# A filtered sequence and its mixture of experts on one core: first group of expert 0 in halves, and another order in the last batch

## The chip, the cores and the metric

The program runs on one core of a Trainium2 chip: TensorE (PE) for matmuls and transposes, VectorE (DVE), ScalarE (ACT), GpSimd (POOL), SyncE (SP) which only issues transfers, and 16 DMA engines. The metric is the device time of one execution in microseconds (us). The times of before are those of three runs, and one further execution was profiled; every row below is from that one.

## What is computed

Eight sequences of 2496 tokens with 256 channels are filtered in the frequency domain, and the result goes through a mixture of eight experts in which every expert takes exactly cap = 2496 tokens, given out in the order of the logits over all tokens:

```python
X = np.fft.rfft(x, axis=1);  Y = X * F[None]          # F = filt_r + 1j * filt_i
y = np.fft.irfft(Y, n=2496, axis=1).reshape(19968, 256)
logits = y @ w_gate
for idx in np.argsort(-logits.flatten()):              # greedy, largest logit first
    tok, e = idx // 8, idx % 8
    if assigned[tok] < 0 and counts[e] < cap:
        assigned[tok] = e; counts[e] += 1
for e in range(8):
    m = assigned == e
    out[m] = np.maximum(y[m] @ w1[e], 0.0) @ w2[e]
```

## The kernel before

**The transforms.** A length of 2496 is split as 39 x 64. Each of the eight batches goes through `s1` (L209) and `s2` (L224), is multiplied with the filter (products `P` and `Q` on VectorE at L230 and L231, their sums on GpSimd at L232 and L233, all in `s2`), is transposed (`tr`, ten tiles `q` per batch, L243), and goes through the first inverse stage `inv1` (L279), whose tile `zt` ScalarE copies (L293) and stores to a scratch tensor `zd` in DRAM (two stores on ScalarE's queue, L296, with two `zt` buffers). The second inverse stage `inv2` loads units `z<-zd` of 120 partitions x 5 x 256 numbers (614 KB; each batch has four such and one of 2 x 256 numbers, 246 KB) on SyncE's queue (L362), multiplies them with `cD` (L395), copies them (L396), and stores `xs<-xo` on ScalarE's queue. The first two batches' units run inside the loop over the batches; those of the other six, 30 units called `rest`, run after the last batch.

**The logits.** They are computed in the frequency domain, ahead of `inv2`: gate products (L252, in `tr`), their copy `vs`, `trv` (L271, a high part `Vh` by ScalarE and a remainder `Vl` by VectorE), and `v1` (L314), `v2` (L330), `v3` (L340) into `lg`. The seven first batches go through `v1` to `v3` together while the last is transformed, the last batch alone behind it. `prep` (L536 to L543, VectorE) makes the routing's first operands `M`, `Gm` and `A` of `lg`.

**The routing.** Eleven threshold rounds (`counts`: matmuls L567 and L580) run among the matmuls of `inv2`; `places` (L758 to L780: one-hot tiles `OH`, matmuls L764, ScalarE pieces `junka` L768, then small VectorE pieces) turns the result into lists of tokens, one list for each chunk of 512 tokens of an expert.

**The experts.** Each expert has five groups of tokens (4 x 512 and 448). GpSimd gathers the rows (`xg`, L823, four gathers per group), `turn` transposes them (L837; two halves of 256 tokens, ScalarE makes the high part `xo` at L840, VectorE the remainder `z` at L841), `first` makes 8 products `pz` of 6 matmuls, 512 columns wide (L859), of which ScalarE makes the relu's high part (L865) and VectorE its remainder (L873), `second` makes `py` (L913, L914), and GpSimd scatters. `split` makes high and low parts of weights (L816, L817). Accumulators `pz` have four buffers.

**What sets the order.** Outside `manual_schedule` the events of `run` are sorted by slot (ten slots to a batch, B = 8 batches) and then by priority, and a scheduler with its own model puts the instructions in each engine's order. Inside `manual_schedule` (from the routing's rounds on) TensorE's order is that of the code, and the other engines' that of the scheduler. `issue_after(x)` has an instruction ordered behind x. `Pump` deals out the routing's pieces by a clock of its own. Between the last `inv2` unit and the first transpose of expert 0, 24 constant matmuls (`rest`, L1015) run.

## Time and profile before

| | |
|---|---|
| runs | 1471.03, 1453.58, 1469.07 us (median 1469.07) |
| profiled execution | 1465.58 us, of which the span from the first instruction to the last is 1463.8 us |
| granted TensorE clock, mean | 0.982 |
| PE busy | 1391.3 us (95%) |
| DVE, ACT, POOL busy | 955.6, 723.7, 663.6 us |
| DMA | 149.17 MB |

Times in rows are in microseconds from the start of the span. A row of a timeline has the start, the duration, the engine, line and operation, output and inputs by the program's names, and, in brackets, how long the engine stood idle before it and what released it. `SPq`, `ACTq` are issues of transfers, whose duration is that of the issuing, not of the transfer.

### The profile page before, as it was taken

The page shows a single profiled execution, that of the slowest core. Times are in us where ns is not written, and L with a number is a line of the kernel's source. Part 1 is how long each engine was busy: PE and PEld are TensorE (multiplying, and loading weights), DVE is VectorE, ACT ScalarE, POOL GpSimd, SP SyncE. Part 2 cuts the span into 40 slices and gives each one's busy share as a digit, 9 for nine tenths or more (in the row PEclk, how much of TensorE's full clock was granted, in tenths as well). Part 3 has the DMA queues.
Part 4 walks back from the last instruction along what each step waited for, and adds up shares of the span by engine and source line. Part 5 has one row for each costly group of instructions (what it writes and reads, how often), then busy time and mean ns, then how long its engine had stood idle before and what let it go on. Part 6 is the DMA issues. An engine that isn't in the chain of part 4 may idle for free. (4 is left out here: it accounts for less than half of the span.)

```text
span 1463.8 us, 24844 instructions
## 1 busy us (share of the span) xinstructions
PE 1391.3 (95%) x9127; PEld 1148.7 (78%) x9127; DVE 955.6 (65%) x2574; ACT 723.7 (49%) x1686; POOL 663.6 (45%) x729
## 2 busy tenths in 40 slices
PE   7899999998997999899999899999999999999998
PEld 6889899776445787677778788787878888888887
DVE  5666676576566789666876976977877854432231
ACT  5666677534473345344544533644553654533332
POOL 5433344243004745553664546366545644445423
PEclk9999999999998999999999999999999999999999
DMA  8554454888892102112110211211211221111100
GB/s 263 185 148 143 126 163 116 237 239 206 328 348 74 51 22 95 53 35 75 59 52 25 98 49 39 90 51 48 95 37 50 102 95 52 38 48 46 42 26 27
DMA packets 54780, 149.17 MB, mean 102 GB/s; under 512 B 9258, under 2 KB 29866, under 8 KB 50706
## 3 DMA queue, kind: packets, MB, share of 16 engines
q0 software_dynamic: 17552, 57.72, 12.1%
q1 hardware_dynamic: 9803, 47.11, 10.6%
q10 hardware_dynamic: 27304, 42.76, 9.5%
q8 instruction: 72, 1.18, 0.3%
q14 instruction: 49, 0.40, 0.1%
HBM read 83.89 MB, written 63.70 MB: 101 GB/s over the span
## 5 line engine op out<-in xcount | busy, mean ns | idle before, releaser
L913 PE MATMUL py<-w,hl 128*128 128x512 f32 x1216 | 445.6, 405 | 0.5 <-ACT hl L865 0.3
L914 PE MATMUL py<-w,hl 128*128 128x256 f32 x1216 | 341.9, 281 | 1.0 <-DVE hl L873 0.6
L865 ACT ACTIVATE hl<-pz 128x512 fp32r<-128x512 f32 (+1 forms) x320 | 186.8, 586 | 214.7 <-PE pz L859 189.0
L859 PE MATMUL pz<-xo,w0h 128*128 128x512 f32 (+1 forms) x640 | 264.4, 413 | 10.3 <-DVE hl L876 3.7
L913 PEld LDWEIGHTS py<-w,hl 128*128 128x128 f32 x1216 | 229.8, 189 | 51.4 <-issue 1.2
L924 POOL TENSOR_TENSOR y<-y 128x256 f32<-128x256 f32 x152 | 122.4, 806 | 311.2 <-ACT y L923 309.9
L859 PE MATMUL pz<-xo,w0l 128*128 128x512 f32 (+1 forms) x640 | 249.9, 390 | 0.0
L859 PE MATMUL pz<-z,w0h 128*128 128x512 f32 (+1 forms) x640 | 249.3, 390 | 0.2 <-issue 0.2
L914 PEld LDWEIGHTS py<-w,hl 128*128 128x128 f32 x1216 | 230.7, 190 | 5.3 <-DVE hl L873 2.2
L873 DVE SCALAR_TENSOR_TENSOR hl<-pz,hl 128x512 fp32r<-128x512 f32 x227 | 155.0, 687 | 116.0 <-ACT hl L865 101.8
L823 POOL DMA_INDIRECT xg<-xs,xid x160 | 168.3, 1052 | 135.8 <-issue 41.0
L923 ACT COPY y<-py 128x512 f32<-128x512 f32 x152 | 89.1, 586 | 282.8 <-PE py L914 188.5
L925 POOL DMA_INDIRECT out<-y,oid x160 | 174.5, 1090 | 48.1 <-POOL y L924 33.6
L859 PEld LDWEIGHTS pz<-xo,w0h 128*128 128x128 f32 x640 | 122.0, 191 | 33.7 <-DVE hl L873 3.8
L232 POOL TENSOR_TENSOR P<-P 128x256 f32<-128x256 f32 x80 | 58.9, 737 | 184.6 <-DVE P L230 184.5
L859 PEld LDWEIGHTS pz<-xo,w0l 128*128 128x128 f32 x640 | 121.3, 190 | 24.1
L859 PEld LDWEIGHTS pz<-z,w0h 128*128 128x128 f32 x640 | 122.0, 191 | 17.3 <-DVE z L841 1.0
L216 ACT COPY Y<-p 64x240 f32<-64x240 f32 (+1 forms) x304 | 116.0, 382 | 30.4 <-PE p L209 19.8
L209 PE MATMUL p<-cS,xr 117*128 117x120 f32 x688 | 100.5, 283 | 7.2 <-DMA xr<-xl 7.1
L559 DVE TENSOR_TENSOR Gm<-M,thr 117x1232 bf16<-117x1232 f32 (+2 forms) x80 | 105.5, 1329 | 0.2
L209 PEld LDWEIGHTS p<-cS,xr 117*128 117x128 f32 x688 | 91.0, 199 | 11.2 <-issue 4.7
L224 PE MATMUL p<-cW,Y 128*128 128x128 f32 x640 | 88.7, 281 | 2.3 <-ACT Y L216 1.5
(229 smaller groups left out, 2274.2 us busy)
## 6 DMA issues: line engine op xcount, KB each, us to landing
zd<-zt ACTq DMA_DIRECT2D x80, 256.0 KB
z<-zd SPq DMA_DIRECT2D x18, 600.0 KB
xs<-xo ACTq DMA_DIRECT2D x18, 600.0 KB
xr<-xl SPq DMA_DIRECT2D x6, 1404.0 KB
xr<-xl SPq DMA_DIRECT2D x7, 1111.5 KB
xr<-zd SPq DMA_DIRECT2D x8, 600.0 KB
xs<-xr ACTq DMA_DIRECT2D x8, 600.0 KB
xs<-Y ACTq DMA_DIRECT2D x6, 600.0 KB
```

The lines of the kernel that those rows point to most:

```text
L209: nc.tensor.matmul(p[:, q-q0, :120], s.xr[b][:, q], s.cS1, start=True, stop=True)
L216: x = (nc.vector.tensor_copy if dve else nc.scalar.copy)(dst, src)
L559: nc.vector.tensor_tensor(Gm[:, s0:s1, :m], s.M[:, s0:s1].unsqueeze(2).to_broadcast([117, s1 - s0, m]), thr[:117].unsqueeze(1).to_broadcas ...
L823: s.lastg = s.nc.gpsimd.indirect_dma_start(out=xg[:n], out_offset=None, in_=s.xs, in_offset=bass.IndirectOffsetOnAxis(ap=ids[0][:n, t:t+1] ...
L859: nc.tensor.matmul(p[:, :n], w[:, sl], x[:, k, :n], start=m == 0, stop=m == 5)
L865: s.lasta = nc.scalar.activation(h[:, :n], p[:, :n], AF.Relu).ins
L873: nc.vector.scalar_tensor_tensor(l[:, :n], p[:, :n], 0.0, h[:, :n].bitcast(F32), op0=OP.max, op1=OP.subtract)
L913: nc.tensor.matmul(pp, hs[g][f][:, hi], w2[:, :, 256*f:256*f+256], start=f == 0, stop=False, skip_group_check=True)
L914: nc.tensor.matmul(pp[:, f % 2], hs[g][f][:, lo], w2h[:, 256*f:256*f+256], start=False, stop=f > 5, skip_group_check=True)
L923: s.lasta = nc.scalar.copy(yy, pp).ins
L924: nc.gpsimd.tensor_tensor(y, y, yy[:, 1], op=OP.add)
L925: st = nc.gpsimd.indirect_dma_start(out=out_rows, out_offset=bass.IndirectOffsetOnAxis(ap=ids[1][:w, 4*g+t:4*g+t+1], axis=0), in_=y[:w], i ...
```

## The change

In the last batch, seven `z` loads that SyncE issued in a row (`rest[0:7]`) are each held by a one-element GpSimd copy into the buffer (`gated_z`), which reads a product of group 0, 1, 2, 3, 3, 4 or 4. The gate products are taken out of `tr` into `gates` and come, with `trv` and `v1`, half a slot after a group's second `s2`, ahead of the transposes; tiles 8 and 9 are transposed later. `v2`, `v3` and `prep` of the last batch move from slot 2.9 behind the loop to 1.0. `prep` of the first seven batches is ordered behind the last `Q` product. The first round's first count matmul is ordered behind the last matmul of `v3`. At the hand-over 34 constant matmuls run instead of 24; the two halves of the first group are transposed apart, with 4 constant matmuls between the two tiles of the first half and 3 behind it; `halves` runs the 8 products of the group twice, 256 columns wide, with the second half transposed at step 4 of the first pass. Routing of the next expert begins 3 units of the pump's clock later, and the weight splits wait until 16 steps are over.

```diff
...
@@ -245,13 +246,19 @@
             nc.scalar.copy(s.y7b(q), p)
         else:
             s.split(b, q, p, nc.vector)
-        if k:
-            p = s.ps.tile([128, 128], F32, name="pv", tag="c", bufs=4)
-            for dh in range(2):
-                for k in range(4):
-                    nc.tensor.matmul(p[32*k:32*k+32], s.gate[:, dh], yt[dh][:, k], start=dh == 0, stop=dh == 1, skip_group_check=True)
-            s.vs[b, g] = s.wp.tile([128, 128], F32, name="vs", bufs=1)
-            nc.scalar.copy(s.vs[b, g], p)
+        if k and b < B - 1:
+            s.gates(b, g)
+
+    def gates(s, b, g):
+
+        nc = s.nc
+        yt = [s.yt[b, g, dh] for dh in range(2)]
+        p = s.ps.tile([128, 128], F32, name="pv", tag="c", bufs=4)
+        for dh in range(2):
+            for k in range(4):
+                nc.tensor.matmul(p[32*k:32*k+32], s.gate[:, dh], yt[dh][:, k], start=dh == 0, stop=dh == 1, skip_group_check=True)
+        s.vs[b, g] = s.wp.tile([128, 128], F32, name="vs", bufs=1)
+        nc.scalar.copy(s.vs[b, g], p)
 
     def y7b(s, q):
         if q == 9 and s.y9 is None:
@@ -337,7 +344,7 @@
         for g0 in range(0, G, n):
             g1 = min(g0 + n, G)
             p = s.pt([128, g1 - g0, c], not b0)
-            nc.tensor.matmul(p[:120], s.cD, s.U[:, g0:g1], start=True, stop=True)
+            s.lastv = nc.tensor.matmul(p[:120], s.cD, s.U[:, g0:g1], start=True, stop=True).ins
             nc.vector.tensor_copy(s.lg[:, b0:b1, g0:g1], p[:117].rearrange("p g (b e) -> p b g e", e=8))
 
     def more_z(s, units):
@@ -360,6 +367,12 @@
             z = s.new_z(True) if (b, t) in s.rest else s.ex[(b + t) % 2]
         s.z[b, t] = z
         s.nc.sync.dma_start(z[:, :g1-g0], s.zd[b].rearrange("a (i g) c -> (a i) g c", i=3)[:, g0:g1])
+
+    def gated_z(s, u, k, g):
+
+        z = (s.zp if k < 3 else s.zw).tile([120, 5, D], F32, name="z", tag="z", bufs=3 if k < 3 else NZ)
+        s.nc.gpsimd.tensor_copy(z[:1, 0, :1], s.yt[B - 1, g, 1][:1, 0, :1])
+        s.load_z(*u, z)
 
     def early(s):
 
@@ -430,9 +443,14 @@
             for g in range(5):
                 for dh in range(2):
                     at(o + 2*g + dh, 1, s.s2, b, g, dh)
-                at(o + 2*g + 4.5, 3.5, s.trv, b, g)
+                if b < B - 1:
+                    at(o + 2*g + 4.5, 3.5, s.trv, b, g)
+                else:
+                    at(o + 2*g + VG, 2.5, s.gates, b, g)
+                    at(o + 2*g + VG + 0.1, 2.5, s.trv, b, g)
+                    at(o + 2*g + VG + 0.2, 2.5, s.v1, g, b, B)
             for q in range(10):
-                at(o + q + 3, 3, s.tr, b, q)
+                at(10*B + 0.8 if b == B - 1 and q > 7 else o + q + 3, 3, s.tr, b, q)
                 if b < B - 1 or q < 2:
                     at(o + q + I1, 4, s.inv1, b, q)
         at(10*B - 20, 0, s.early)
@@ -442,20 +460,22 @@
         at(10*B - 9.5, 0, freed)
         for g in range(5):
             at(10*B - V1 + g*V1D, 3.8, s.v1, g, 0, B - 1)
-            at(10*B - 5.2 + 2*g, 3.6, s.v1, g, B - 1, B)
         at(10*B - V2, 3.8, s.v2, 0, B - 1)
         at(10*B - V3, 3.8, s.v3, 0, B - 1)
-        at(10*B - VP, 3.8, prep, 0, G * (B - 1))
+        def early_prep():
+            with s.tc.issue_after(s.lq):
+                prep(0, G * (B - 1))
+        at(10*B - 0.7, 3.8, early_prep)
         def act():
             s.cps = (s.nc.scalar.copy,) * 2
         at(10*B - AC, 0, act)
-        for u in rest[:3]:
-            at(10*B - min(3, I2 - 5.6), 9, s.load_z, *u)
+        for k, g in enumerate(ZG):
+            at(10*(B - 1) + 2*g + 1.5, 9, s.gated_z, rest[k], k, g)
         at(10*B - 0.8, 9, s.more_z, rest[3+NZ:9+NZ])
         at(10*B + 2.9, 3.61, s.more_z2, rest[9+NZ:3+NZ+MZ])
-        at(10*B + 2.9, 3.6, s.v2, B - 1, B)
-        at(10*B + 2.9, 3.62, s.v3, B - 1, B)
-        at(10*B + 2.9, 3.64, prep, S - G, S)
+        at(10*B + VE, 2.6, s.v2, B - 1, B)
+        at(10*B + VE, 2.62, s.v3, B - 1, B)
+        at(10*B + VE, 2.64, prep, S - G, S)
         for q in (2, 3, 4):
             at(10*B + 2.9, 3.7 + 0.01 * q, s.inv1, B - 1, q)
         for e in sorted(ev, key=lambda e: e[:3]):
@@ -564,7 +584,8 @@
         last = (S - 1) // b
         for k in range(last + 1):
             w = min(b, S - b*k) * n
-            nc.tensor.matmul(c[:KL, :w], s.Gm[:, K*k:K*k+KL], s.A[:, b*n*k:b*n*k+w], start=k == 0, stop=k == last, skip_group_check=True)
+            with s.tc.issue_after(s.gate) if made and k == 0 else nullcontext():
+                nc.tensor.matmul(c[:KL, :w], s.Gm[:, K*k:K*k+KL], s.A[:, b*n*k:b*n*k+w], start=k == 0, stop=k == last, skip_group_check=True)
         t1 = s.wp.tile([128, 128], F32, name="t1", bufs=2)[:K, :b*n].rearrange("p (e s) -> p e s", s=b)
         D1 = s.wp.tile([128, 8], F32, name="D1", bufs=2)[:K, :n]
         XT = s.XT[nj].pop(0)
@@ -832,6 +853,8 @@
         w = 0
         for t in range(2):
             n = min(128, CAP - 128*(4*g+2*h+t))
+            if t and s.warm:
+                s.warm()
             x = s.xg[e, 4*g+2*h+t].rearrange("p (k q) -> p k q", k=2)
             for k in range(2):
                 nc.tensor.transpose(p[:, k, 128*t:128*t+n], x[:n, k], s.id[:n, :n])
@@ -886,10 +909,34 @@
                             hook(('g', g + 2))
                 yield from first(g, f)
 
+        def halves():
+            hs[0] = [s.wp.tile([128, 1024], F32R, name="hl", bufs=NH) for _ in range(8)]
+            xh, xl = s.xT[e, 0]
+            for h in range(2):
+                for f in range(8):
+                    if h == 0 and f == 4:
+                        s.turn(e, 0, 1)
+                    if h and f == TF[0]:
+                        s.turn(e, 1, 0)
+                    if h and f == TF[1]:
+                        s.turn(e, 1, 1)
+                        hook(('g', 2))
+                    p = s.ps.tile([128, 256], F32, name="pz", tag="c", bufs=4)
+                    m = 0
+                    for k in range(2):
+                        sl = slice(1024*k+128*f, 1024*k+128*f+128)
+                        for w, x in ((w1h, xh), (w1h, xl), (w1l, xh)):
+                            nc.tensor.matmul(p, w[:, sl], x[:, k, 256*h:256*h+256], start=m == 0, stop=m == 5)
+                            m += 1
+                        yield 0.34
+                    hi, lo = (hs[0][f][:, c:c+256] for c in (256*h, 512+256*h))
+                    s.lasta = nc.scalar.activation(hi, p, AF.Relu).ins
+                    s.lastd = nc.vector.scalar_tensor_tensor(lo, p, 0.0, hi.bitcast(F32), op0=OP.max, op1=OP.subtract).ins
+
         hook(('g', 1))
         for g in range(5):
             n = min(512, CAP - 512*g)
-            yield from firsts(g, 8)
+            yield from halves() if e == g == 0 else firsts(g, 8)
             if g == 4:
                 hook('last')
             if g == 0:
@@ -957,10 +1004,6 @@
             R.cp, R.wp = (pool(st, n, side="right", reuse_waits="tile") for n in ("rc", "rw"))
             R.setup()
             f.zw = pool(zst, "zw", side="right", reuse_waits="tile")
-            f.nload = 3
-            for u in rest[3:NZ+3]:
-                f.load_z(*u)
-            f.nload = 0
         f.late = lambda: nc.sync.dma_start(cD, i['cD'])
         f.run(fc, fw, fx, ps, freed, R.prep, rest)
 
@@ -986,6 +1029,7 @@
                 nxt = k + 3 + NZ + MZ if k < 3 + NZ else k + 3 + NZ
                 if (k < 3 + NZ or k >= 3 + NZ + MZ) and nxt < len(rest):
                     f.load_z(*rest[nxt])
+        R.gate = f.lastv
         pump = Pump(R)
         split = []
         def weights(e):
@@ -1010,9 +1054,11 @@
                 pump.feed(c if c else 0.8)
             for c in units:
                 pass
+            def warm(n):
+                for _ in range(n):
+                    nc.tensor.matmul(p, R.ones16[:117], R.iota, start=True, stop=True)
             p = ps.tile([128, 512], F32, name="rest", tag="b", bufs=2)
-            for _ in range(24):
-                nc.tensor.matmul(p, R.ones16[:117], R.iota, start=True, stop=True)
+            warm(34)
 
         zst.close()
         W.wp = pool(st, "ffp", reuse_waits="tile")
@@ -1025,17 +1071,17 @@
         gather(0, 0)
         with tc.issue_after(W.lastg):
             W.load(1)
-        for h in range(2):
-            R.last = W.turn(0, 0, h)
-        with tc.issue_after(R.last):
-            while split:
-                W.split(*split.pop(0))
+        pump.due = max(pump.due, pump.clock + 3)
         n = 0
         def flush(p):
             while split and split[0][1] < p:
                 with tc.issue_after(W.lasta):
                     W.split(*split.pop(0))
         with tc.manual_schedule(engines={mybir.EngineType.PE}):
+            W.warm = lambda: warm(4)
+            R.last = W.turn(0, 0, 0)
+            W.warm = None
+            warm(3)
             for e in range(8):
                 pump.limit = e + 1
                 def hook(what):
@@ -1050,10 +1096,12 @@
                         else:
                             W.turn(e + 1, 0, what - 1)
                 for pe in W.run(e, pump, hook):
+                    if n < 16:
+                        R.last = W.lastd or R.last
                     pump.feed(pe)
                     n += 1
 
-                    if split and n % PACE == 0:
+                    if split and n % PACE == 0 and n > 16:
                         with tc.issue_after(W.lasta):
                             W.split(*split.pop(0))
 
```

**SyncE, transfers issued around the end of the last batch** (`zd_k` are the scratch tensors, `z`, `cW`, `F`, `Vh` and `Vl` the buffers that the units are loaded into). Before:

```order
L362 DMA z<-zd_62 120x1280
L362 DMA z<-zd_62 120x512
L362 DMA z<-zd_63 120x1280 x2
L362 DMA z<-zd_62 120x1280 x3
L362 DMA cW<-zd_64 120x1280 x2
L362 DMA F<-zd_63 120x1280 x2
L362 DMA F<-zd_63 120x512
L362 DMA F<-zd_64 120x1280
L362 DMA Vh<-zd_64 120x1280
L362 DMA Vl<-zd_64 120x512
```

and now:

```order
L369 DMA z<-zd_62 120x1280 x4
L369 DMA z<-zd_62 120x512
L369 DMA cW<-zd_64 120x1280 x2
L369 DMA F<-zd_63 120x1280 x2
L369 DMA F<-zd_63 120x512
L369 DMA F<-zd_64 120x1280
L369 DMA z<-zd_63 120x1280 x2
L369 DMA Vh<-zd_64 120x1280
L369 DMA Vl<-zd_64 120x512
```

Two of the seven loads into `z` have moved behind the `cW` and `F` loads; the five ahead of them are issued as their GpSimd copies allow.

**VectorE, the last products of the last batch** (L536 to L543 are `prep`; L230 and L231 the products, L274 makes `Vl` of one group). Before:

```order
L536 TENSOR_REDUCE M<-lg 117x154
L265 TENSOR_TENSOR yl<-pa,yh 128x512
L230 TENSOR_TENSOR P<-p_4151,F 128x512
L231 TENSOR_TENSOR Q<-p_4151,F 128x512
L537 TENSOR_TENSOR Gm<-M,ic 117x462
L539 TENSOR_TENSOR tmp<-lg,M 117x1232
L274 TENSOR_TENSOR Vl<-pv,Vh 128x4x8
L540 TENSOR_TENSOR tmp<-tmp,val 117x1232
L274 TENSOR_TENSOR Vl<-pv,Vh 128x4x8
L541 TENSOR_REDUCE ar<-tmp 117x154
L542 SCALAR_TENSOR_TENSOR ar<-asg,ar 117x154
L543 TENSOR_TENSOR A<-ar,row 117x1232
```

and now, with the lines of the changed kernel (L231 and L232 are the products, L556 to L563 `prep`, L281 makes `Vl`):

```order
L231 TENSOR_TENSOR P<-p_4187,F 128x512
L232 TENSOR_TENSOR Q<-p_4187,F 128x512
L556 TENSOR_REDUCE M<-lg 117x154
L272 TENSOR_TENSOR yl<-pa,yh 128x512
L281 TENSOR_TENSOR Vl<-pv,Vh 128x4x8
L557 TENSOR_TENSOR Gm<-M,ic 117x462
L559 TENSOR_TENSOR tmp<-lg,M 117x1232
L560 TENSOR_TENSOR tmp<-tmp,val 117x1232
L281 TENSOR_TENSOR Vl<-pv,Vh 128x4x8
L561 TENSOR_REDUCE ar<-tmp 117x154
L562 SCALAR_TENSOR_TENSOR ar<-asg,ar 117x154
L563 TENSOR_TENSOR A<-ar,row 117x1232
```

Before, the last `Vl` is the row behind these, after `A`; now it stands behind the second `tmp`, and the first pass of `prep` behind the last `Q`.

**ScalarE, from the last stores of inv2 to the first relu of expert 0** (`w0h` are weight splits, `xo<-ptr` the high part of transposed tokens, `junka` a piece of `places`, `hl` the relu). Before:

```order
L399 DMA xs<-xo 120x1280
L635 CAST X_0_3665<-ru 32x63
L399 DMA xs<-xo 120x512
L816 CAST w0h<-wr_5071 128x512 x4
L840 CAST xo<-ptr 128x2x256 x2
L816 CAST w_5075<-wr_5072 128x512 x4
L865 ACTIVATE hl<-pz 128x512 x3
```

and now:

```order
L412 DMA xs<-xo 120x1280
L409 COPY xo<-pv 120x512
L412 DMA xs<-xo 120x512
L837 CAST w0h<-wr_5078 128x512 x4
L863 CAST xo<-ptr 128x2x256
L789 ACTIVATE junka,js<-rt,loc 128x176 x4
L933 ACTIVATE hl<-pz 128x256 x4
L863 CAST xo<-ptr 128x2x256
L933 ACTIVATE hl<-pz 128x256 x5
```

Four pieces of `places` that stood among the copies of `inv2` now stand ahead of the first relu, and only half of the tokens' high part.

**VectorE, the same place.** Before:

```order
L841 TENSOR_TENSOR z<-ptr,xo 128x2x256 x2
L644 TENSOR_REDUCE M<-lg 117x176
L646 TENSOR_TENSOR tmp<-lg,M 117x1408
L559 TENSOR_TENSOR Gm<-M,ic 117x528
L817 TENSOR_TENSOR w_5075<-wr_5072,w_5075 128x512 x3
L648 TENSOR_TENSOR tmp<-tmp,val 117x1408
L817 TENSOR_TENSOR w_5075<-wr_5072,w_5075 128x512
L873 SCALAR_TENSOR_TENSOR hl<-pz,hl 128x512 x3
L650 TENSOR_REDUCE ar<-tmp 117x176
L841 TENSOR_TENSOR z<-ptr,xo 128x2x256
L873 SCALAR_TENSOR_TENSOR hl<-pz,hl 128x512
```

and now (L864 makes the tokens' remainder, L934 that of a half product, L665 and L667 are passes of the routing):

```order
L794 SCALAR_TENSOR_TENSOR xid<-ex,js 128x4
L797 TENSOR_TENSOR t_5089<-js,row 128x28
L800 TENSOR_TENSOR t_5279<-js,ex 128x4
L934 SCALAR_TENSOR_TENSOR hl<-pz,hl 128x256
L799 TENSOR_REDUCE t1b<-t_5089 128x4
L934 SCALAR_TENSOR_TENSOR hl<-pz,hl 128x256
L801 SCALAR_TENSOR_TENSOR oid<-t1b,t_5279 128x4
L934 SCALAR_TENSOR_TENSOR hl<-pz,hl 128x256 x2
L665 TENSOR_REDUCE M<-lg 117x176
L864 TENSOR_TENSOR z<-ptr,xo 128x2x256
L934 SCALAR_TENSOR_TENSOR hl<-pz,hl 128x256 x2
L667 TENSOR_TENSOR tmp<-lg,M 117x1408
```

The routing's passes now come after the fourth remainder; ahead of these rows stand the tokens' remainder of the first half and seven more pieces of `places`.

## Rows read from the trace of the kernel before

**Rows 1.** Waits of TensorE, 280 to 470: line, releaser: us, times, longest.

```profile
PE pv L395 <- ACT xo L396: 4.5, 2, 2.6
PE pa L279 <- ACT zt L293: 2.5, 1, 2.5
```

**Rows 2.** Busy by stretch: us, engines, clock, DMA share, GB/s.

```profile
325.00:335.00 10.00, 6.28 (x65) 5.15 (x64) 6.83 (x12) 3.93 (x9) 2.88 (x4) 1.00 0.61 160
332.40:440.00 107.60, 95.57 (x518) 56.21 (x516) 66.95 (x224) 60.60 (x139) 10.95 (x10) 0.95 0.88 297
...
345.00:355.00 10.00, 9.13 (x49) 8.24 (x50) 3.71 (x12) 3.34 (x7) 2.52 (x2) 0.66 0.71 173
360.00:398.00 38.00, 37.30 (x186) 20.44 (x183) 22.66 (x75) 18.15 (x39) 1.59 (x1) 1.00 0.94 344
398.00:410.00 12.00, 9.44 (x33) 4.72 (x32) 5.32 (x19) 5.78 (x12) 0.00 (x0) 0.86 0.77 223
...
448.00:467.00 19.00, 16.68 (x69) 13.05 (x70) 18.75 (x31) 9.84 (x24) 2.69 (x3) 0.88 0.20 73
467.00:1463.00 996.00, 966.87 (x5688) 798.05 (x5686) 652.13 (x1915) 446.54 (x997) 511.17 (x507) 0.99 0.17 56
```

**Rows 3.** Timeline of SyncE, end of the last batch.

```profile
306.41 7.42 SPq L362 DMA_DIRECT2D z<-zd  x7
332.43 0.77 SPq L362 DMA_DIRECT2D cW<-zd  x2
```

**Rows 4.** Timeline of ScalarE, 312 to 335.

```profile
315.46 2.28 ACTq L296 DMA_DIRECT2D zd<-zt  x2
...
327.06 0.58 ACT L293 COPY zt<-pa 128x512 f32<-128x512 f32 x1 [5.24 <-DMA zd<-zt]
```

**Rows 5.** Timeline of VectorE, 325 to 347.

```profile
332.78 1.43 DVE L536 TENSOR_REDUCE M<-lg 117x154 f32<-117x1232 f32 x1
334.12 0.68 DVE L265 TENSOR_TENSOR yl<-pa,yh 128x512 fp32r<-128x512 f32 x1
...
335.31 0.68 DVE L231 TENSOR_TENSOR Q<-p,F 128x512 f32<-128x512 f32 x1
...
341.92 1.44 DVE L543 TENSOR_TENSOR A<-ar,row 117x1232 bf16<-117x1232 f32 x1
```

**Rows 6.** Timeline of TensorE, 322 to 360.

```profile
327.70 0.39 PE L279 MATMUL pa<-yh,cEh 128*128 128x256 f32 x1 [2.50 <-ACT zt L293]
...
353.76 1.12 PE L395 MATMUL pv<-z,cD 120*120 120x512 f32 x2
```

**Rows 7.** Timeline of TensorE, end of inv2 and first transposes.

```profile
432.82 5.34 PE L1015 MATMUL rest<-iota,ones 117*128 117x512 f16 x24
443.23 0.66 PE L837 MATMUL ptr<-id,xg 128*128 128x128 f32 x2 [5.06 <-DMA xg<-xs,xid]
```

**Rows 8.** Timeline of GpSimd, 412 to 470.

```profile
440.32 0.96 POOL L823 DMA_INDIRECT xg<-xs,xid  x1 [20.86 <-DMA xs<-xo]
```

**Rows 9.** Timeline of TensorE, first matmuls of expert 0.

```profile
448.24 0.79 PE L859 MATMUL pz<-xo,w0h 128*128 128x512 f32 x1 [0.68 <-ACT xo L840]
...
466.50 0.39 PE L913 MATMUL py<-w,hl 128*128 128x512 f32 x1
```

**Rows 10.** Timeline of ScalarE, last units of inv2.

```profile
429.92 0.43 ACT L768 ACTIVATE junka<-rt,loc 128x176 bf16<-128x176 f32 x1
```

**Rows 11.** Timeline of VectorE: a 336-column copy, then the hand-over.

```profile
331.63 0.50 DVE L341 COPY lg<-pv 117x336 f32<-117x336 f32 x1
...
445.80 0.69 DVE L841 TENSOR_TENSOR z<-ptr,xo 128x512 fp32r<-128x512 f32 x1 [8.04 <-ACT xo L840]
448.22 0.69 DVE L841 TENSOR_TENSOR z<-ptr,xo 128x512 fp32r<-128x512 f32 x1 [1.73 <-ACT xo L840]
448.82 1.61 DVE L644 TENSOR_REDUCE M<-lg 117x176 f32<-117x1408 f32 x1
...
456.58 1.88 DVE L873 SCALAR_TENSOR_TENSOR hl<-pz,hl 128x512 fp32r<-128x512 f32 x3
```

More of the change, by code (lines that the diff above doesn't have):

```diff
@@ L26 @@
 I1, EZ = 5, 0.8
-V1, V1D, V2, V3, VP, I2, AC = 8, 0.5, 3, 2, -1, 5, 6.5
+V1, V1D, V2, V3, AC = 8, 0.5, 3, 2, 6.5
+VG, VE, ZG = 2.5, 1.0, (0, 1, 2, 3, 3, 4, 4)
 NP, NZ, MZ, NXO, ZB, NH = 5, 4, 8, 4, 2, 10
@@ L793, in __init__ @@
         s.scat = []
-        s.wt, s.xg, s.xT = {}, {}, {}
+        s.wt, s.xg, s.xT, s.lastd, s.warm = {}, {}, {}, None, None
     def weights(s, e, widx):
```

## Prediction

> **What bounds the kernel now.** TensorE is busy for almost the whole program, so what can be won lies in the places where it waits or runs at the lower clock. The first view to read is therefore the table of TensorE's waits between 280 and 470 us, the only stretch whose order changes much [rows 1]: one wait of 2.5 us on a `zt` copy, and 4.5 us in two on `xo` copies, the longest 2.6. The second view is busy time by stretch [rows 2]. [...] From 325 to 335 TensorE has 6.28 us of work in 10 and the DMA share falls to 0.61: a stall. [...] From 360 to 398 TensorE is full at clock 1.00, but the DMA share is 0.94 too: loads and stores of `inv2` run almost as tightly as the matmuls. From 448 to 467 VectorE has 18.75 us of work in 19: the hand-over is VectorE's. After 467 come 996 us of experts whose TensorE order the change leaves alone.
>
> Then the timelines of single engines. SyncE issues seven `z` loads in a row, over 7.42 us from 306.41 [rows 3]. Two `zt` stores are issued at 315.46 behind them; ScalarE's next `zt` copy, which needs their buffer, starts at 327.06 after 5.24 us of waiting for `zd<-zt`, and TensorE goes on at 327.70 after 2.50 us idle [rows 4, 6]. On VectorE the first pass of `prep` (1.43 us at 332.78) stands ahead of the last `P`/`Q` pair, and the last `Q` is at 335.31 [rows 5]. The first `z` matmul after all this is at 353.76 [rows 6].
>
> **Part 1, the last batch.** The stall: seven loads are 6 x 614 KB and one of 246 KB, 3.9 MB. The stores issued 9 us after the first of them took 327.06 - 315.46 = 11.6 us to give the buffer back [rows 4]. Afterwards five loads are each held by a GpSimd copy behind one group's product and two stand behind the `cW` and `F` loads, so a store finds one or two loads of 614 KB before it, at most 2/6 of that queue: 11.6 us shrinks to perhaps 4, and the wait of 2.5 us goes. Removing the `prep` pass from ahead of the last product gives back 334.12 - 332.78 = 1.34 us (the next piece on that engine starts at 334.12 [rows 5]). With the 2.5 us of the stall the last `Q` comes 3.8 us earlier, at about 331.5.
>
> The tail behind it: before, from the last `Q` to the first `z` matmul, 353.76 - 335.31 = 18.4 us. The `Vl` of group 4 stands behind `A` (start 341.92, 1.44 us [rows 5]), 8.0 us after `Q`; in the new order it stands behind the second `tmp` pass, so it need not wait for two passes of about 1.4 us (the maximum and `A`) and a small one of 0.3, but the first pass (1.34) and a `yl` (0.6) now come after `Q` and not before: 8.0 - 2.8 - 0.3 + 1.3 + 0.6 = 6.8, 1.2 us better. The chain then is as before: `v1`, `v2`, `v3`, 18 `inv1`. Nine count matmuls go from inside `v1` to behind `inv1` and cancel. The gates and `v1` of the earlier groups already lie before the last `Q`, for which I take 0.5 us more: 18.4 - 1.2 - 0.5 = 16.7. So the first `z` matmul comes at 331.5 + 16.7 = 348.2: TensorE gains 5.6 us (3 if the waits on `vs` and `Vh` merely move, 8 if the clock stays at 1.00 through `inv1`).
>
> What the DMA makes of it: from 332.4, the first `cW` load, to 440 the share is 0.88 of 107.6 us, 94.7 us of transfers [rows 2]. Loads that lay in the stretch to 325 are now partly behind it: four of the seven, 2.0 MB, at 297 GB/s 6.9 us, less about 2.7 that the idle share of 325 to 335 absorbs: 4.2 us. At 0.94, the best long stretch, 98.9 us take 105.2. The `cW` buffers come free some 2.5 us earlier, at 330, and so the last store lands at 435 to 436 instead of 440. I take 4.5 us, not 5.6; bounds 1 (the transfers absorb it all but the stall's end) to 8. The seven one-element GpSimd copies, each below one of its products (2.88 us for four, 0.72 each [rows 2]), lie in that engine's gaps and cost nothing; were it full, they would cost 7 x 0.72 = 5 us, but it has 2.88 us of work in 10.
>
> [...]
>
> **Part 2, the end of inv2.** Two one-hot products and the four ScalarE pieces that read them leave the last units for the hand-over. A piece is 0.43 us [rows 10], with its read-out about 0.6 by estimate, 2.4 us of ScalarE in all, with the copies of the last stores queued behind them. If the stores wait for the DMA anyway nothing is won, if for ScalarE all of it: -0.5 us (0 to -2.4), nearer the first since the share there is high.
>
> **Part 3, the hand-over.** Let G be the first gather's issue, 440.32, released by the stores [rows 8]. Before: first transposes G+2.9 after 5.06 us idle, first `pz` G+7.9, first `py` G+26.2 [rows 7, 9]. The warm matmuls take 5.34 us for 24 [rows 7], so 34 take 7.6 of the 10.4 us between 432.82 and 443.23, and 2.9 us stay empty. Idle gaps bear both ways: the stretch with the 2.50 us gap at 327.70 kept clock 1.00, the one from 398 to 410 with the gap of 2.6 had 0.86 [rows 1, 2, 6]. If the first `pz` run at full clock, the 0.88 of 448 to 467 becomes 1.00: at most 0.12 x 19 = 2.3 us of TensorE, which is not what bounds here.
>
> Only the first half's 256 tokens are needed to begin, so `pz` may start two transposes and one ScalarE/VectorE pair earlier: 2.0 to 2.4 us. But four ScalarE pieces now stand ahead of the first relu: they need an `OH` that VectorE makes after `z`, and 2.4 us of ScalarE. From `z` of half 0 (445.8): 0.6, two small, `OH` 0.7, two products, four pieces 2.4: first relu at 449.3 at the earliest, 1.1 us after the first `pz` of before began.
>
> Then VectorE. Its work up to the eighth remainder before: 18.75 us in the 19 to 467 [rows 2]. After: eight remainders of 0.60 us pitch (three take 1.88 [rows 11]) become sixteen of 256 columns. The trace has none; a lower bound is half of 0.60, 0.30, an upper one the 0.50 us row of 336 columns [rows 11]; between them the two rows fall by 0.18 us for 176 columns, which at 256 gives 0.42, less the 0.06 by which pitch is below duration: 0.36. 16 x 0.36 - 8 x 0.60 = +1.0 us (0 to +3.2). The places of chunk 1, about 2.3 us of small pieces and an `OH`, come in too. Against it: routing's passes (1.61 us each [rows 11]) start only after four remainders, the 1.73 us that VectorE stood idle before its second `z` [rows 11] fill up, and it starts at 445.8 rather than 448.2. 1.0 + 2.3 - 1.7 - 2.0 = -0.4: the first `py` stays near G+26. Term: 0 (-2 to +2).
>
> [...]
>
> **Part 4, the experts.** Order unchanged on TensorE after the first group; some weight splits one place later on VectorE, which has 652 us of work in 996 [rows 2]. Nothing, +-2.
>
> **Sum.** -4.5 - 0.5 + 0 + 0 = -5.0 us, on the profiled execution's 1465.58: 1460.6. That execution lies 3.5 us below the median shown, 1469.07; the same change on the median gives 1464.1. I take **1462**.
>
> **Rivals.** (a) *All of part 1 arrives*: `inv2` is bound by TensorE's chain (98% busy from 360 to 398 [rows 2]), the transfers keep up, and the clock holds through `inv1` and the first `pz`: -8 - 1 = 1456. For: a 2.6 us TensorE wait on `xo` [rows 1] that an earlier start may leave out. Against: share 0.94. (b) *The DMA absorbs it*: the moved 2 MB, without cover, keep the last store at 439 to 440: -0.5, 1465. For: the share; 6.9 us of transfers moved are more than the 5.6 us gained. Against: 12% of the stretch was idle [rows 2]. (c) *Slower*: at the hand-over the four pieces and VectorE's longer list hold the relus; four product buffers then stop TensorE. If a 256-column remainder costs 0.5 us (+3.2 instead of +1.0) and chunk 1's gathers, now behind its places, land after the second half wants its transposes at about G+17, the first `py` comes at G+30: +4, which with (b)'s part 1 gives 1469. It decides from a remainder of 0.42 us. (d) *The stall is not the loads'*: the zt wait stays, since the store's own 512 KB were slow; then only the 1.3 us of `prep` remain: 1464. Against: of all the `zt` stores from 280 on, this is the one that TensorE waits for [rows 1].
>
> **Chances.** Forecast 0.45, (a) 0.13, (b) 0.22, (c) 0.13, (d) 0.07. About 2% (29 us) is what a measurement of this kernel can tell from no change; none of these cases reaches it. Since executions of before spread from 1453.6 to 1471.0, the range takes the changes -4 on the lowest and 0 on the highest: 1450 to 1471; the forecast's own is 1456 to 1467. Faster 0.02, same 0.96, slower 0.02.
>
> **What would show it.** Right: no wait on `zt` near 327; the first `z` matmul near 348; DMA share from 345 to 400 above 0.9; the first gather near 435; first relu of the halves about 9 us after the gather; first `py` 25 to 27 after it, and 997 us from there to the end. Wrong: a gather as late as 440 with TensorE waiting on `z` or `xo` (b); a first `py` past G+29 (c); or a gather before 433 (a).

## Result and profile after

The changed kernel takes 1465.58 us (median of 22 executions, 1451.89 to 1473.80), the kernel before 1455.94 us (median of 22, 1445.96 to 1471.03): a ratio of 1.0068, 95% interval 1.0047 to 1.0088. It is about 10 us slower, where 5 us of gain were forecast. The ratios here and below leave out executions that lie more than 1.5% above the fastest of their kernel.

The two profiled executions stand the other way round: a span of 1457.0 us for the changed kernel, 1463.8 for the one before. Executions of one kernel lie up to 25 us apart. Up to the first `s2` matmul of the last batch the change does nothing, and there the two already lie 8.9 us apart; busy time by stretch, before and after:

```profile
0.00:286.42 286.42, 267.64 (x2476) 246.00 (x2477) 185.87 (x343) 189.47 (x488) 116.04 (x170) 0.97 0.58 170
```

```profile
0.00:277.49 277.49, 261.94 (x2475) 240.10 (x2476) 184.47 (x343) 190.64 (x488) 115.72 (x170) 0.99 0.61 176
```

The column behind the last bracket is the granted clock: 0.97 against 0.99. So everything below is measured from a mark inside the same trace. The marks are the first `s2` matmul of the last batch, the end of the last `Q`, the first `z` matmul, the first gather and the first `py`. Busy time between them (columns as in [rows 2]), before, with the stretch from 30 to 50 us behind the first mark as the last line:

```profile
286.42:335.99 49.57, 44.72 (x414) 36.49 (x413) 34.79 (x67) 18.41 (x44) 18.57 (x36) 1.00 0.83 235
335.99:353.76 17.77, 14.78 (x138) 12.46 (x136) 10.11 (x19) 7.18 (x15) 2.59 (x4) 0.81 0.84 203
353.76:440.32 86.56, 77.92 (x344) 41.47 (x342) 53.25 (x201) 51.32 (x119) 6.69 (x5) 0.98 0.88 318
440.32:466.50 26.18, 18.88 (x74) 13.75 (x75) 18.94 (x29) 10.53 (x24) 8.54 (x9) 0.80 0.24 81
316.42:336.42 20.00, 16.00 (x153) 13.18 (x153) 13.57 (x24) 5.31 (x13) 7.39 (x11) 1.00 0.79 218
```

and after:

```profile
277.49:326.62 49.13, 45.49 (x437) 37.23 (x435) 34.13 (x66) 19.13 (x44) 19.26 (x41) 1.00 0.69 188
326.62:342.22 15.60, 12.79 (x111) 11.23 (x112) 11.30 (x19) 7.28 (x17) 2.85 (x6) 0.89 0.97 232
342.22:438.49 96.27, 81.80 (x350) 43.40 (x348) 50.19 (x189) 49.60 (x110) 6.10 (x6) 0.95 0.90 310
438.49:465.78 27.29, 21.32 (x134) 17.58 (x134) 19.62 (x49) 13.98 (x40) 8.52 (x9) 0.87 0.25 78
307.49:327.49 20.00, 19.13 (x192) 16.14 (x188) 14.55 (x25) 7.60 (x17) 8.40 (x15) 1.00 0.51 130
```

Line by line: the last `Q` comes 0.4 us earlier, the tail behind it is 2.2 us shorter, the stretch from the first `z` matmul to the gather is 9.7 us longer, and the hand-over 1.1 us. In sum 180.08 us became 188.29. The last lines show where the DMA engines were left empty: a share of 0.51 where before had 0.79.

Of the 9.7 us, 3.9 are longer busy time of TensorE (81.8 us against 77.9, at a granted clock of 0.95 against 0.98) and 5.8 are more idle time (14.5 against 8.6). What the engine waited for, from 280 to 470 us (line, releaser: us, times, longest; [rows 1] has before):

```profile
PE pv L408 <- ACT zt L300: 7.4, 1, 7.4
PE pv L408 <- ACT xo L409: 5.3, 3, 2.8
PE ptr L860 <- DMA xg<-xs,xid: 3.8, 1, 3.8
```

The `zt` wait of 2.5 us is gone, and one of 7.4 us is there. Behind these 7.4 us without work the clock was lower: the granted clock is 0.81 from 357.8 to 368.0, 1.00 from 342.2 to 350.4, and the two matmuls of 342.22 take 1.12 us, the two that follow the wait 2.06. Its place shows in the timelines of SyncE, ScalarE and TensorE:

```profile
301.38 22.17 SPq L369 DMA_DIRECT2D z<-zd  x5
323.88 1.84 SPq L369 DMA_DIRECT2D cW<-zd  x2
326.64 1.68 SPq L369 DMA_DIRECT2D F<-zd  x4
329.58 0.77 SPq L369 DMA_DIRECT2D z<-zd  x2
333.21 0.32 SPq L369 DMA_DIRECT2D Vh<-zd  x1
335.63 0.32 SPq L369 DMA_DIRECT2D Vl<-zd  x1
```

```profile
341.74 0.58 ACTq L303 DMA_DIRECT2D zd<-zt  x1
342.37 0.63 ACTq L303 DMA_DIRECT2D zd<-zt  x1
...
357.14 0.59 ACT L300 COPY zt<-pa 128x512 f32<-128x512 f32 x1 [9.36 <-DMA zd<-zt]
```

```profile
342.22 1.12 PE L408 MATMUL pv<-z,cD 120*120 120x512 f32 x2
...
357.78 2.06 PE L408 MATMUL pv<-z,cD 120*120 120x512 f32 x2 [7.37 <-ACT zt L300]
```

With two buffers a copy needs the stores of the pair before the last. Before, that was not the pair of 315.46 which the prediction named but this one, issued amid the seven loads [rows 3, 4] and 17.6 us ahead of the copy of 327.06 (ScalarE, before):

```profile
309.45 0.58 ACTq L296 DMA_DIRECT2D zd<-zt  x1
310.08 0.71 ACTq L296 DMA_DIRECT2D zd<-zt  x1
```

Now five loads are issued over 22 us and the last two 6 us behind the first `cW` load, so ten loads (`cW` to `Vl`) stand in the 12 us from 323.88. The stores of 341.74 give their buffer back at 357.14, 15.4 us later, and hold up ScalarE, in whose queue the `xo` copies of `inv2` stand too. It is the same kind of wait three pairs of stores later, three times as long for TensorE.

### The profile page after: what moved, and what is told of

Read it like the earlier page. It is cut to its first block, busy times and chain, and to the rows that moved or that the text cites. A ratio compares the mean times of both kernels' runs of the same rounds, so it can differ in the third digit from the quotient of the medians.

```text
span 1457.0 us, 25012 instructions
## 1 busy us (share of the span) xinstructions
PE 1386.8 (95%) x9192; PEld 1144.7 (79%) x9192; DVE 956.5 (66%) x2582; ACT 727.3 (50%) x1694; POOL 667.6 (46%) x736
## 5 line engine op out<-in xcount | busy, mean ns | idle before, releaser
L888 ACT ACTIVATE hl<-pz 128x512 fp32r<-128x512 f32 (+1 forms) x312 | 182.4, 587 | 205.0 <-PE pz L882 191.5
L882 PE MATMUL pz<-xo,w0h 128*128 128x512 f32 (+1 forms) x624 | 255.7, 410 | 6.7 <-DVE hl L899 1.8
L882 PE MATMUL pz<-xo,w0l 128*128 128x512 f32 (+1 forms) x624 | 241.8, 388 | 0.0
L882 PE MATMUL pz<-z,w0h 128*128 128x512 f32 (+1 forms) x624 | 241.1, 386 | 0.1
L896 DVE SCALAR_TENSOR_TENSOR hl<-pz,hl 128x512 fp32r<-128x512 f32 x219 | 149.6, 686 | 112.9 <-ACT hl L888 112.1
L882 PEld LDWEIGHTS pz<-xo,w0h 128*128 128x128 f32 x624 | 117.7, 189 | 28.5 <-ACT junka L789 4.1
L882 PEld LDWEIGHTS pz<-xo,w0l 128*128 128x128 f32 x624 | 117.3, 188 | 23.2
L882 PEld LDWEIGHTS pz<-z,w0h 128*128 128x128 f32 x624 | 117.8, 189 | 15.7 <-DVE z L864 0.8
```

The source lines that it names most:

```text
L882: nc.tensor.matmul(p[:, :n], w[:, sl], x[:, k, :n], start=m == 0, stop=m == 5)
L888: s.lasta = nc.scalar.activation(h[:, :n], p[:, :n], AF.Relu).ins
L896: nc.vector.scalar_tensor_tensor(l[:, :n], p[:, :n], 0.0, h[:, :n].bitcast(F32), op0=OP.max, op1=OP.subtract)
```

## The experiments

Every kernel was timed beside the kernel before on the same chip. "Row" are the seven loads issued in a row, "held" those held by GpSimd copies ("six": one load fewer), "zt" is the number of `zt` buffers. "Wait" is TensorE's longest wait on `zt` from the first `s2` of the last batch to the gather, "Q to G" runs from the end of the last `Q` to the first gather, "G to py" from there to the first `py` (starts of trace rows, one profiled execution each). R is the ratio of times to before with its 95% interval.

| kernel | loads | order, hand-over | zt | wait | Q to G | G to py | R |
|---|---|---|---|---|---|---|---|
| before | row | old, old | 2 | 2.5 | 104.3 | 26.2 | 1 |
| changed | held | new, new | 2 | 7.4 | 111.9 | 27.3 | 1.0068 (1.0047 to 1.0088) |
| e1_ungated | row | new, new | 2 | none | 104.9 | 25.3 | 0.9938 (0.9896 to 0.998) |
| e2_gated_only | held | old, old | 2 | 4.4 | 109.5 | 26.1 | 1.0054 (1.0022 to 1.0086) |
| e3_old_handover | held | new, old | 2 | 5.7 | 111.9 | 26.9 | 1.0046 (1.0014 to 1.0079) |
| e4_handover_only | row | old, new | 2 | 1.6 | 105.4 | 27.3 | 1.001 (0.9974 to 1.0045) |
| e6_order_only | row | new, old | 2 | none | 102.8 | 26.2 | 0.9985 (0.9954 to 1.0015) |
| f1_gate_early | held, group 0 | new, new | 2 | none | 105.1 | 26.4 | 1.0025 (0.9988 to 1.0062) |
| f2_gate_late | held, groups 3, 4 | new, new | 2 | none | 110.4 | 27.2 | 1.0077 (1.0043 to 1.0111) |
| f3_two_late | five at 0, two at 4 | new, new | 2 | 6.7 | 113.9 | 26.9 | 1.0052 (1.0018 to 1.0086) |
| f4_places_ahead | row | new, new, places early | 2 | none | 104.6 | 22.8 | 1.0038 (1.0007 to 1.0069) |
| g2_gated_zt2 | held, six | new, new | 2 | 5.4 | 110.2 | 26.3 | 1.003 (0.9997 to 1.0063) |
| g1_gated_zt3 | held, six | new, new | 3 | none | 104.8 | 27.2 | 0.9919 (0.9897 to 0.9942) |
| g3_ungated_zt3 | row | new, new | 3 | none | 102.5 | 26.8 | 0.9938 (0.9915 to 0.9962) |
| h1_before_zt3 | row | old, old | 3 | none | 103.3 | 26.1 | 0.989 (0.9864 to 0.9916) |
| h3_gated_only_zt3 | held, six | old, old | 3 | none | 102.5 | 26.2 | 0.9879 (0.985 to 0.9909) |
| h4_gated_zt3_again | held, six | new, new | 3 | 0.2 | 103.1 | 27.3 | 0.9931 (0.9907 to 0.9955) |

### One part at a time

My first theory was that of bytes: the held loads leave the DMA engines empty, and what is not moved then has to be moved later. Its rivals were the order and the hand-over. e1 puts the loads back in a row:

```diff
-        for k, g in enumerate(ZG):
-            at(10*(B - 1) + 2*g + 1.5, 9, s.gated_z, rest[k], k, g)
+        for u in rest[:3]:
+            at(10*B + 0.6, 9, s.load_z, *u)
...
             f.zw = pool(zst, "zw", side="right", reuse_waits="tile")
+            f.nload = 3
+            for u in rest[3:NZ+3]:
+                f.load_z(*u)
+            f.nload = 0
```

> The changed kernel with its seven z loads put back in a row, as before; the new order of the last batch and the new hand-over stay. Measured from the first s2 matmul of the last batch to the first gather, before took 153.9 us and the changed kernel 161.0. Backlog theory (the held loads leave the DMA engines empty from 30 to 50 us after that matmul, 10.2 us of transfers there instead of 15.9, and the rest lands later, in front of the zt stores): 150 to 154 here, the transfers of 30 to 50 us back to about 16 us, no wait of 7 us on zt near the start of inv2; the whole 4 to 8 us faster than the changed kernel. Order theory (the earlier matmuls meet a transfer-bound inv2, whatever the loads do): 159 to 162, no faster. Hand-over theory: 161 stays or not, but the time from gather to first py is what costs, and the whole stays some 8 us above before.

From the first `s2` to the gather it took 153.75 us and had no `zt` wait: the 7.3 us are back. From the first `z` matmul to the gather TensorE was as busy as in the changed kernel, at a granted clock of 0.94 against 0.95, and the stretch is 7.0 us shorter:

```profile
349.30:438.54 89.24, 82.50 (x350) 43.13 (x348) 50.87 (x189) 50.27 (x111) 6.51 (x6) 0.94 0.89 311
```

So the difference between these two is idle time. The pair of stores that cost the wait is issued at 348.32 here, 17.7 us behind the first `cW` load (17.9 in the changed kernel), with eight loads in that time and not ten, and the copy that needs its buffer starts without a wait (ScalarE):

```profile
348.32 1.25 ACTq L303 DMA_DIRECT2D zd<-zt  x2
...
353.58 0.59 ACT L300 COPY zt<-pa 128x512 f32<-128x512 f32 x1
```

Its ratio says 0.9938, but by all its twelve executions the median is 1460.95 against 1463.53, so I read it as not slower than before, and no more than that. e2 makes the reverse edit in the kernel before:

```diff
-        for u in rest[:3]:
-            at(10*B - min(3, I2 - 5.6), 9, s.load_z, *u)
+        for k, g in enumerate(ZG):
+            at(10*(B - 1) + 2*g + 1.5, 9, s.gated_z, rest[k], k, g)
...
-            f.nload = 3
-            for u in rest[3:NZ+3]:
-                f.load_z(*u)
-            f.nload = 0
```

> The kernel before with only the seven z loads held by the GpSimd copies. Backlog theory: first s2 matmul to first gather 158 to 162 us instead of 153.9, transfers of 30 to 50 us after that matmul about 10 us instead of 15.9, the whole 4 to 8 us slower than before. Order theory and hand-over theory: 153 to 155, the whole as before within 2 us; it might even gain the 2.5 us of the first zt wait.

157.6 us to the gather (0.4 under the forecast range) and 1.0054. TensorE's wait in that kernel:

```profile
PE pa L280 <- ACT zt L294: 4.4, 1, 4.4
```

e4 takes the change's hunks on the hand-over alone, e6 those on the order alone:

```diff
+            yield from halves() if e == g == 0 else firsts(g, 8)
...
+            warm(34)
...
```

> The kernel before with only the new hand-over (34 constant matmuls, first group of expert 0 in halves, later routing and splits). First gather to first py was 26.2 us before (of it 5.1 us lost to the lower clock) and 27.3 after (3.4 lost). Backlog theory: 153 to 154.5 to the gather, 26 to 28 from there, the whole within 3 us of before. Hand-over theory: the whole 6 us or more above before.

```diff
+                    at(o + 2*g + VG, 2.5, s.gates, b, g)
...
+            with s.tc.issue_after(s.lq):
+                prep(0, G * (B - 1))
...
```

> The kernel before with only the new order of the last batch (gates ahead of transposes, prep behind the last product, first counts behind v3); loads and hand-over as before. Backlog theory: first s2 matmul to first gather 150 to 154 us, the whole 0 to 4 us faster than before. Order theory: 159 to 162, the whole 5 us or more slower.

153.9 us and 27.3 from the gather for e4, 152.1 and 26.2 for e6; neither is apart from before by more than its interval. So the held loads are the loss, and in e6 the `zt` wait of before is gone too, with the loads still in a row: under the new order alone the copy starts 17.5 us behind the stores that it needs (323.43 behind 305.96), and has not waited. Both rivals fall. e3 has held loads and new order with the old hand-over (the hunks of e4 undone):

> The changed kernel with the hand-over of before: held loads and new order of the last batch stay. Backlog theory: first s2 matmul to first gather 159 to 162 us, gather to first py 26.0 to 26.5, the whole 5 to 9 us above before: the held loads cost more beside the new order (7.3 us) than alone (3.7), with or without the hand-over. If the 3.5 us between those two came from the hand-over: 156 to 158.

159.4 us to the gather, 26.9 from it (0.4 over), 1.0046: the hand-over hardly matters for it. By the stretches, one execution each, the held loads cost more beside the new order (159.4 against e6's 152.1) than alone (157.6 against 153.9); by R, 1.0046 and 1.0054, that is not shown.

### How late, and how many

```diff
-VG, VE, ZG = 2.5, 1.0, (0, 1, 2, 3, 3, 4, 4)
+VG, VE, ZG = 2.5, 1.0, (0, 0, 0, 0, 0, 0, 0)
```

> The changed kernel with all seven z loads held for group 0's product alone, so they come about 4 us later than in the kernel before and all ahead of the cW loads; copies, buffers, order and hand-over as in the change. First s2 matmul of the last batch to first gather: 161.0 us in the changed kernel, 153.8 with the loads in a row. Backlog theory: 153 to 156 us, bytes moved in the first 40 us about 10 MB (7.9 in the changed kernel), zt stores of the early inv2 without a 10 us gap, the whole 4 to 8 us below the changed kernel. If instead the GpSimd copies or the other buffers' order cost the time: 159 to 162.

To the gather 158.9 us, over the forecast, but the surplus lies ahead of the last `Q` (53.7 us instead of 49.1); from there it took 105.1 and no `zt` wait. So the copies and the buffers' order cost nothing behind `Q`. What lengthened the stretch ahead of it, and whether the later loads did, one execution doesn't show. The other way:

```diff
-VG, VE, ZG = 2.5, 1.0, (0, 1, 2, 3, 3, 4, 4)
+VG, VE, ZG = 2.5, 1.0, (3, 3, 4, 4, 4, 4, 4)
```

> The changed kernel with the seven z loads held for group 3 (two) and group 4 (five), so five stand behind the cW and F loads. Backlog theory: still fewer bytes in the first 40 us (about 7 MB), first s2 matmul to first gather 163 to 168 us, the zt wait at the start of inv2 longer than 7.4 us. If the number of late loads doesn't matter because the inverse stage is bound by its matmuls: 161, as in the changed kernel.

161.1 us: no more than the changed kernel, though five loads instead of two are late. The bytes theory in its simple form failed here, and the `zt` wait that it forecast is not there either. TensorE waited on `xo` copies instead, between 353.9 and 447.8 for 10.0 us, twice the 4.9 us of e1 in the same part:

```profile
PE pv L408 <- ACT xo L409: 10.0, 6, 2.8
```

And with five prompt and only the last two late:

```diff
-VG, VE, ZG = 2.5, 1.0, (0, 1, 2, 3, 3, 4, 4)
+VG, VE, ZG = 2.5, 1.0, (0, 0, 0, 0, 0, 4, 4)
```

> The changed kernel with five loads held for group 0 alone (some 4 us later than in a row) and two for group 4, so that only these two stand behind the cW and F loads. Backlog theory: the 1.2 MB of two loads missing in the first 40 us, last Q product to first gather 106 to 109 us, between 105 (all early) and 111.9 (the change). If the five spread loads alone cost: 104 to 106.

113.9 us, past the forecast of 106 to 109: two late loads cost as much as the seven spread ones. Waits of TensorE and of ScalarE there:

```profile
PE pa L286 <- ACT zt L300: 6.7, 1, 6.7
```

```profile
ACT zt L300 <- DMA zd<-zt: 9.1, 1, 9.1
```

So in f3 and the changed kernel not the sum of late bytes decides but what stands in front of one pair of stores. f2 is not explained by that: from the last `Q` to the gather it lost 5.5 us to e1 without a `zt` wait of TensorE, and no run gave it a third buffer.

### The wait or the bytes

A third `zt` buffer is meant to let ScalarE and TensorE go on while a store is late, with the loads in the same order. It needs room, for which one `zw` buffer goes, and so one held load; g2 is the partner with that alone.

```diff
-VG, VE, ZG = 2.5, 1.0, (0, 1, 2, 3, 3, 4, 4)
-NP, NZ, MZ, NXO, ZB, NH = 5, 4, 8, 4, 2, 10
+VG, VE, ZG = 2.5, 1.0, (0, 1, 2, 3, 3, 4)
+NP, NZ, MZ, NXO, ZB, NH = 5, 3, 8, 4, 3, 10
```

> The changed kernel with three zt buffers instead of two, and three zw buffers instead of four to make room, so six held loads instead of seven (groups 0, 1, 2, 3, 3, 4). Last Q product to first gather was 111.9 us in the changed kernel and 104 to 105 with the loads in a row. If the cost is the wait itself (a zt buffer whose store landed late stops ScalarE and TensorE, 7.4 us, though the transfers could follow): the wait goes and 104 to 107 us remain. If the cost is the bytes that weren't moved earlier: the wait goes or moves to z or xo, and 109 to 113 us remain.

> The partner of the run with three zt buffers: the changed kernel with three zw buffers and six held loads, but two zt buffers as in the change. Either theory: the zt wait is there, about 5 to 8 us, and last Q product to first gather is 109 to 113 us, the whole some 5 to 10 us above before. If it is 105 or less, one load more or less in front decides, and not the hold.

104.8 us against 110.2 from the last `Q` to the gather, 0.9919 against 1.003. Of the 15.3 us between their medians this stretch holds 5.4. TensorE's wait with two buffers, and what is left of ScalarE's with three:

```profile
PE pa L286 <- ACT zt L300: 5.4, 1, 5.4
```

```profile
ACT zt L300 <- DMA zd<-zt: 0.2, 1, 0.2
```

The bytes theory falls for this change: the same held loads and the same late bytes cost little once the buffer is there (104.8 us against 102.5 with the loads in a row in g3, and 103.1 in h4, which is the kernel of g1 once more). With the loads in a row and three buffers:

> Three zt buffers and three zw buffers with the z loads in a row, new order and new hand-over kept. Last Q product to first gather 103 to 106 us, as with two zt buffers and the loads in a row, since no zt wait of more than 1 us stands there; the whole within 3 us of before. If the third buffer lets the stores of the early inverse stage run ahead, 100 to 103.

102.5 us, below the forecast by 0.5, and 0.9938, lower than "within 3 us" (9 us). Little of the surplus lies in the last batch (152.7 us from its first `s2` to the gather, before 153.9), which raised the question whether before was limited by the same two buffers. h1 is before with the `NP` line of the edit above, h3 adds the held loads, h4 is g1 again beside them:

> The kernel before with three zt buffers and three zw buffers, nothing of the change. If the zt buffers were the limit all along: no zt wait near the end of the last batch (2.5 us before) and none of the waits on zt in the first seven batches (5.2 us in the profile of before), the first s2 matmul of the last batch some 4 to 6 us earlier, the whole 5 to 12 us below before. If the third buffer only helps the changed order: within 3 us of before.

> The kernel before with three zt and three zw buffers and six held loads, without the new order and hand-over. Wait theory: with the third buffer the hold costs nothing, the same as the kernel before with three zt buffers within 3 us, last Q product to first gather 103 to 106 us. Bytes theory: 4 us or more slower than that kernel, 108 to 111.

> The changed kernel with three zt and three zw buffers and six held loads, beside the kernel before with the same buffers on the same chip. If order and hand-over are worth nothing net: within 3 us of it. If the earlier first z matmul reaches the end: 3 to 6 us below it.

h4 lies 4.7 us above h1, on neither side that was expected. 0.989, 0.9879 and 0.9931 on one chip (medians 1448.31, 1446.60 and 1452.98 against 1462.89). The hold is worth nothing either way when nothing waits for the stores (0.9879 and 0.989 lie in each other's intervals), and the order and hand-over have no gain to show on top (0.9931 against 0.9879; the intervals just overlap). Where the 14.6 us of h1 lie is shown in part. From the first `s2` of the last batch to the gather it took 150.3 us, before 153.9. TensorE's waits up to that mark, before and h1:

```profile
PE p L209 <- DMA xr<-xl: 7.1, 7, 2.6
PE pa L279 <- DVE zt L293: 5.2, 2, 3.1
PE pv L271 <- DVE zt L293: 2.4, 1, 2.4
...
PE pv L252 <- DVE zt L293: 0.3, 1, 0.3
```

```profile
PE p L209 <- DMA xr<-xl: 8.0, 4, 3.1
...
PE pv L252 <- DVE zt L293: 0.3, 1, 0.3
```

7.9 us of waits behind `zt` became 0.3, and h3 has 0.3 too. But the changed kernel, with two buffers, has only 3.7 us of them there and reaches the mark at 277.49, h1 at 277.40: how much of the gain is these waits, single executions don't settle. By their ratios both h1 and h3 beat the kernel before and the changed one.

### The hand-over's pieces

f4 is e1 with the places of chunk 1 dealt out among the last `inv2` units, as before:

```diff
-            while (0, 0) not in pump.tags:
+            while (0, 1) not in pump.tags:
```

> The changed kernel with the z loads in a row again, and with the places of chunk 1 dealt out among the last inv2 units, as before, so that their four ScalarE pieces and one-hot tile don't stand ahead of the first relu. First s2 matmul to gather 152 to 155 us. Gather to first py: 27.3 in the changed kernel, 25.3 with the loads in a row. If those pieces hold the first group: 22.5 to 24.5 us and the whole 5 us below before. If VectorE's list as a whole does: 25 to 26 us and no gain over the kernel with the loads in a row.

22.8 us from the gather to the first `py`, 2.5 to 4.5 less than the others: the four pieces do hold the first group. But the whole was 1.0038, not 5 us below before, and e1, which differs from it in this alone, had 0.9938 on another chip. Where the 3 us won ahead of `py` go is not settled: its execution had 993.4 us from the first `py` to the end of the last, against 992.5 before and 986.4 in the changed kernel; the mean granted clock of these whole executions was 0.983, 0.982 and 0.991.

## Why the prediction was wrong

**The last `Q` 3.8 us earlier: wrong.** It came 0.4 us earlier. The 2.5 us wait did go and the `prep` pass did move, but the step left out that gates, `trv` and `v1` now stand ahead of the transposes and so ahead of that `Q`; in the tail I counted this as 0.5 us of gain and did not count the price in front of it. TensorE's work up to the last `Q` rose from 44.72 to 45.49 us in the stretches shown above, and a wait of 1.1 us for `Vl` is new there. Another 1.5 us are one execution's and not the step's: a wait for a load into `xr` 6 us behind the mark, ahead of everything that was moved, took 1.8 us instead of 0.3 (1.3 in h1, where nothing was moved).

**The tail: right.** From the end of the last `Q` to the first `z` matmul 15.6 us instead of 17.8, 2.2 us better against 1.7.

**"A store finds one or two loads before it ... and the wait of 2.5 us goes": the step that failed.** It asked only about the one pair of stores whose wait [rows 4] show, and took the wrong pair for it. The later pairs use the same two buffers, and two of the seven loads had been put in front of one of them: the pair of 341.74 follows ten loads and not "one or two", and its buffer took 15.4 us to come back, not "perhaps 4". I had a row that shows how long a store behind loads can take (11.6 us by my reading, 17.6 by the right pair, shown above) and the order that shows the two loads behind `F`, and did not put them together. What is late next was asked of the bytes (a share of 0.94, 4.2 us of backlog) and not of the queue. The price was 7.4 us of waiting, and from the first `s2` of the last batch to the gather +7.1 instead of -5.

**Rival (b) came nearest and was too mild.** It had the gain lost, not turned into a loss, and by the wrong mechanism: with three buffers the same bytes cost 2.3 us at most (g1 against g3). The rival on the other side, (c), put the loss at the hand-over, which cost 1.1 us (0 was forecast, up to 2). Rival (d) has half a point: the wait of before was not the seven loads' alone, since e6 loses it with the loads in a row.

**The hand-over: right in its parts.** First relu 9.5 us after the gather (9.0 forecast), no earlier `py`. A 256-column remainder, which no row showed, takes 0.42 us, two 0.75, so a pitch of 0.33 (0.36 taken); timelines of ScalarE and VectorE after:

```profile
448.02 1.14 ACT L933 ACTIVATE hl<-pz 128x256 fp32r<-128x256 f32 x3
```

```profile
448.82 0.42 DVE L934 SCALAR_TENSOR_TENSOR hl<-pz,hl 128x256 fp32r<-128x256 f32 x1
...
449.65 0.75 DVE L934 SCALAR_TENSOR_TENSOR hl<-pz,hl 128x256 fp32r<-128x256 f32 x2
```

**The base.** I put the sum on one execution of 1465.58 us and three runs with a median of 1469.07; the median of 22 is 1455.94. The forecast of 1462 and its range of 1450 to 1471 hold the 1465.58 of the changed kernel, but only because the base stood 10 us too high: that is luck. Nor is 2% the least that can be told from no change: the interval here reaches 0.2% to either side, and the loss of 0.7% is clear of it.

## What to carry to other kernels

When a wait is traced to a transfer that stands behind others, follow the whole queue of the waiting resource (here two buffers and every store through them) and not only the one wait: here the loads moved out of one store's way stood in a later one's. The cheap cure was a buffer more (TensorE's wait on `zt` was 5.4 us in g2 and is not there in g1); it took one line and one load buffer, and was worth more than the whole rearrangement (0.9919 in g1, 1.003 in g2, 1.0068 for the change). And compare stretches from a common mark: the profiles of one execution each pointed the wrong way here.

## What the runs showed of the hardware

With two loads of 614 KB more in front of it (ten and not eight since the first `cW` load), a pair of 256 KB stores on another engine's queue gave its buffer back after 15.4 us in the changed kernel, and within 5.3 us in e1. With only these two loads late (f3) the delay was the same as with all seven spread: ScalarE waited 9.1 us in f3 and 9.4 in the changed kernel. Five late loads (f2) cost no more than the two of the changed kernel, 110.4 against 111.9 us from the last `Q` to the gather.

The granted clock differed between kernels, but not by the buffers alone. Over all timed executions it was 0.989 (g1) and 0.988 (g3) with three `zt` buffers against 0.980 for before on that chip, and 0.985 (h1), 0.986 (h3) and 0.988 (h4) against 0.981 on another; with two buffers g2 had 0.983, but e1 0.987 against 0.981 and f1 0.986 against 0.983. In the profiled executions of the kernels with three buffers the first `s2` of the last batch came at 267.5 to 277.4 us, elsewhere at 277.5 to 287.6. How much of this is the clock's and how much the waits', these runs do not tell apart.
